# The first keys' tile is loaded earlier and the first unit's maxima are computed among the last projections

## The chip, the cores and the metric

The kernel runs on one core of one Trainium2 chip. The metric is the device time of one execution in microseconds (us); lower is better. The core has TensorE (PE; its weight loads are shown as PEld), VectorE (DVE), ScalarE (ACT), GpSimd (POOL) and SyncE (SP), which here issues nearly all transfers. Each engine works through a queue of its own in order, and semaphores order the engines among each other.

## The reference

Two independent parts read their own inputs, and their outputs are joined on the last axis. L is 2048, D is 448, N is 256, H is 16 heads of 28.

```python
# part A: a diagonal state space convolution
dt = exp(log_dt);  A = -exp(log_A_real) + 1j * A_imag;  C = (C_real + 1j * C_imag) * dt[:, None]
P = exp((A * dt[:, None])[:, :, None] * arange(L))
K = 2.0 * einsum("dn,dnl->dl", C, P).real
y = irfft(rfft(K, 2 * L) * rfft(u.T, 2 * L))[:, :L].T + u * D_skip
# part B: multi-head attention
q, k, v = split(x @ wqkv)
o = softmax(q @ k.T / sqrt(28)) @ v          # for each head
out = concatenate([y, o @ wo], axis=-1)
```

## The kernel before

The attention runs in 16 units, each one head group of 4 heads (g) and a quarter of 512 queries (c). A softmax needs the maximum of each row of scores ahead of the exponentials. The maxima of unit u + 1 are computed while unit u is in its loop, and their negatives are written as two more rows into the q tile of the unit (`qhat<-mh`), so that the score matmul subtracts them. The first unit has no unit ahead of it, so its maxima are computed before the loop starts.

The program has two stages. In the loop (from line 878) the order is written out by hand and kept on all engines. Ahead of it lies a first stage (lines 213 to 565) in which a list scheduler orders the instructions by their place in the program, by their priority and by when their inputs are ready; the builder writes that order into the queue of each engine. Two lines of work share the engines there:

- *Projections.* `work` holds 48 jobs, twelve for each quarter c of the rows of x: eight `qk_proj` (k and q of each head group) and four `v_proj`. A job is 12 matmuls into one of three PSUM buffers (`pm`, handed out by `w_tile`), since x and the weights are split into a high and a low part (`xh`, `xl`; `w_g`, `vh`, `vl`). Its evacuation (`evac`, kept in `pend` until the next job's matmuls are in the program) writes high and low parts into `hl`, or v into one of two tiles `vst`, and stores them to DRAM. For k of the first two quarters it also makes the difference `dhl` by way of `kb`. In the last quarter the v jobs come first.
- *Seeds.* For part A, eight blocks o = 0..7 go through the thirteen steps that `seeds` lists: transposes of `nat`, phases and their reduction (`tri`), sines (the cosine is `sg<-tri,half_pi`), sizes by Exp, products on GpSimd, `g_first` on VectorE, and two stores, `sd<-qhat` and `sd<-sg`. Two `tri` and two `sg` buffers are in turn.

`slots` gives each step of a seed block its stage (four stages from block to block), and `PW` spreads the 48 jobs over 37 stages. `ahead` adds loads at given stages: the key differences `kdif` from stage A0 = 26, the first unit's q at A1 = 34, the first group's k tiles `khat` at the stages KW. The weights of q and k lie in the tile `k0_t`, which is also the first keys' tile: its part j can only be loaded when all projections of head group j are done.

After that stage the first unit's maxima follow (lines 539 to 563): 16 groups of 128 queries of one head. A group has five matmuls of 512 columns into four PSUM banks. The keys are taken in two halves: `kdif` holds differences of keys in pairs, and max(a, b) is relu(a - b) + b. So a group is one Relu over 128x1024 on ScalarE and one custom VectorE instruction that adds, and keeps the maximum. GpSimd supplies -q (`nq`). `max_end` transposes and splits the maxima, `max_put` sends them, and the loop starts. Its first ScalarE copy, `e<-sdb`, reads the first block's seeds back from DRAM.

In the profile every instruction bears line 76, that of the helper through which all engines are called, so the work is told apart by its tiles.

Of the kernel before, what the change touches and what calls it, by code (L numbers as in the profile page):

```python
# [17 lines left out]
L = 2048  # L18
# [22 lines left out]
PS = 1  # L41
SGB, XB, XL = 2, 5, 4
K0, KP, KD, UP = 0, 3.5, 4, 3
A0, A1, KW = 26, 34, (33, 35, 36)

N1 = 32
N2 = 64
# [44 lines left out]
def body(ctx, tc, a, out):  # L92
# [41 lines left out]
    k0_p = pool(k0_st, "k0_p", side="right")  # L134
    k0_t = k0_p.tile([128, HG, L], F32R, name="khat")

    def mm32(o, w, x_, start, stop, at=0):

# [5 lines left out]
    kt_g, kd_g, q_u, m_u, mh_u, o_u, rl_u = {}, {}, {}, {}, {}, {}, {}  # L144

    def load_k(g, j, p):
        if j == 0:
            t = k0_t if g == 0 else p.tile([128, HG, L], F32R, name="khat")
# [62 lines left out]


    with ExitStack() as st:
        sst, xst, wst, mst, psx, psm = (ExitStack() for _ in range(6))
        t_p = pool(sst, "t_p")
        s_p = pool(sst, "s_p")
        x_p = pool(xst, "x_p")
        y_p = pool(wst, "y_p", side="right")
# [17 lines left out]
        nc.gpsimd.memset(k0_t[:CK].rearrange("p g (n e) -> p (g n) e", e=32)[:, :, DH:].bitcast(F32), 0.0)  # L236
# [14 lines left out]
        nats = {}  # L251

        def load_nat(o):
            nats[o] = s_p.tile([PO, 4, 256], F32, name="nat", bufs=2)
# [178 lines left out]
        def transposes(c):  # L433
            for k in range(NCK):
                pt = ps_t.tile([128, CQ], F32, name="pt")[:CK]
                for t in range(4):
                    nc.tensor.transpose(pt[:, t * 128:(t + 1) * 128], xns[c, t // 2][:, t % 2, k * CK:(k + 1) * CK], ident)
                xh[k] = x_p.tile([CK, CQ], F32R, name="xh", bufs=XB)
                xl[k] = x_p.tile([CK, CQ], F32R, name="xl", bufs=XL)
                nc.scalar.activation(xh[k], pt, AF.Copy)  # L440
                nc.vector.tensor_tensor(xl[k], pt, xh[k].bitcast(F32), ALU.subtract)

        def qk_proj(c, s, g):
            pp = w_tile()
# [30 lines left out]
        def v_proj(c, t):  # L475
# [11 lines left out]
                nc.sync.dma_start(v_d[c][:, :, t], vs.rearrange("p (g h) e -> p g (h e)", g=G))  # L487
            return evac

        work = []  # L490
# [20 lines left out]
        for i in range(2):  # L511
            ahead[A1 + i].append(lambda i=i: load_q(0, range(2 * i, 2 * i + 2)))

        for j, t in enumerate(KW):
            ahead[t].append(lambda j=j: load_k(0, j, k0_p))

        def project():

            e = work.pop(0)() if work else None
            while pend:  # L520
                pend.pop(0)()
            if e:
                pend.append(e)

        for t in range(n_stage):
            while work and n_work - len(work) < n_work * (t + 1) / PW:
                project()
            for f in slots[t] + ahead.get(t, []):
                f()
            if t + 1 == PW:  # L530
                project()
                wst.close()
                load_k(0, HG - 1, k0_p)
# [5 lines left out]
        m_p = pool(mst, "m_p")  # L539
        ps_2 = pool(psm, "ps_2", 4, PSUM)  # L540
        nq = m_p.tile([128, HG, CQ], F32R, name="nq")
        m_u[0, 1] = q_p.tile([128, HG * 4], F32, name="m1", bufs=2)
        for i in range(16):
            j, t = divmod(i, 4)
            ts = slice(t * 128, (t + 1) * 128)
            q, kt = q_u[0][:, j, ts], kt_g[0][j]
            if t == 0:
                nc.gpsimd.tensor_scalar(nq[:, j], q_u[0][:, j].bitcast(F32), -1.0, None, op0=ALU.mult)
            pd, pb = (ps_2.tile([128, 2, CQ], F32, name="p2") for _ in range(2))
            kb = kt.rearrange("p (c s n) -> p c s n", c=NQ, s=2)[:, :2, 1, :]  # L550
            mm = nc.tensor.matmul
            mm(pd[:, 0], q, kd_g[0, j], start=True, stop=True)
            mm(pd[:, 1], q, kt[:, 2 * CQ:3 * CQ], start=True, stop=False)
            mm(pd[:, 1], nq[:, j, ts], kt[:, 3 * CQ:], start=False, stop=True)
            mm(pb[:, 0].rearrange("p (c n) -> p c n", c=2), q, kb, start=True, stop=True)
            mm(pb[:, 1], q, kt[:, 3 * CQ:], start=True, stop=True)
            rl = m_p.tile([128, 2, CQ], F32, name="rl2", bufs=2)
            nc.scalar.activation(rl, pd, AF.Relu)
            nc.vector.tensor_tensor_reduce(rl, pb, rl, 1.0, -3.0e38, ALU.add, ALU.max, m_u[0, 1][:, i:i + 1])
        nc.scalar.activation(half_pi[:1], half_pi[:1], AF.Exp)  # L560
        max_end(0, ps_2.tile([128, 2, CQ], F32, name="p2")[:, 0])
        max_put(0)
        psm.close()
        mst.close()
        sst.close()


# [6 lines left out]
    ps_st = ExitStack()  # L574
    ps_g = pool(ps_st, "ps_g", 1, PSUM)
    ps_w[0] = pool(ps_st, "ps_m", 1, PSUM)
    k_pools = [k0_p, kq_p]

    late = [False]

# [577 lines left out]
```

## Time and profile before

| | us |
|---|---|
| median of 3 runs | 1303.82 (1302.89 to 1305.15) |
| the profiled execution | 1307.74 |
| its span, first to last instruction | 1305.7 |
| evacuation of the 43rd projection (k of head group 1, last quarter) on ScalarE | 181.32 |
| first Relu of the maxima | 211.73 |
| end of the last maximum | 235.65 |
| first copy of seeds in the loop | 245.15 |

The profile shows one execution; its 1307.74 us are 3.92 above the median. A row of the timeline is start, duration, engine, line, operation, output tile <- input tiles, shapes and count, and in brackets the idle time ahead of it with what ended it. A row of the waits is who waited for whom, with total, count and longest in us. Matmuls are pipelined, so their durations overlap and their starts give the pace.

### The profile page before, as it was taken

What the parts mean: (1) busy time and instruction counts of PE and PEld (TensorE: products, weight loads), DVE (VectorE), ACT (ScalarE), POOL (GpSimd) and SP (SyncE); (2) the same over time, 40 slices, a digit from 0 to 9 for tenths busy, and PEclk for the clock granted to TensorE, in tenths of its full rate; (3) what the DMA queues carried; (4) which work ended last, traced back from release to release, by engine and by line L of the source; (5) the groups of instructions that cost most, each with busy time, mean ns of one, the idle gap of its engine ahead of it and who ended that gap; (6) DMA issues with size and microseconds to landing.
All of it is one profiled execution on the core that took longest, in us unless ns stands there. A gap on an engine that the chain in (4) does not pass through costs nothing.

```text
span 1305.7 us, 32148 instructions
## 1 busy us (share of the span) xinstructions
PE 1228.7 (94%) x12193; PEld 695.7 (53%) x12193; DVE 907.0 (69%) x2001; ACT 980.3 (75%) x2046; POOL 865.9 (66%) x684
## 2 busy tenths in 40 slices
PE   6888877799999999999999999999997999999998
PEld 5766755355555555555555555555554555545333
DVE  5676656677777787777788888888986555636111
ACT  4877875588888888888788888888886666756463
POOL 2677654478888788888769999999995221424421
PEclk9989887799999999999999999999999999999999
DMA  6677679735866455468634232743324453647666
GB/s 202 207 273 257 218 259 271 212 66 136 185 147 142 109 149 157 142 169 231 162 104 105 56 83 62 157 111 78 82 59 139 146 158 136 203 142 238 202 161 175
DMA packets 200082, 205.28 MB, mean 157 GB/s; under 512 B 95992, under 2 KB 158520, under 8 KB 197880
## 3 DMA queue, kind: packets, MB, share of 16 engines
q1 hardware_dynamic: 199864, 203.22, 56.1%
q8 instruction: 96, 1.57, 0.5%
q14 instruction: 58, 0.48, 0.1%
q10 hardware_dynamic: 64, 0.02, 0.0%
HBM read 120.74 MB, written 82.18 MB: 155 GB/s over the span
## 4 chain that ended last, share of the span: by engine, by line
PE 72%; POOL 8%; ACT 7%; DVE 5%; DMA 4%; issue 4%; SPq 0%; ACTq 0%; POOLq 0%
PE pm L76 39%; PE pss L76 16%; PE po L76 16%; POOL sg L76 2%; POOL e L76 2%; DMA khat<-k 2%; POOL tri L76 2%; ACT tri L76 1%; ACT sg L76 1%; DVE mx L76 1%; POOL p L76 1%; ACT L76 1%; ACT p L76 1%; POOL eu L76 1%; DVE rl L76 1%
## 5 line engine op out<-in xcount | busy, mean ns | idle before, releaser
L76 ACT ACTIVATE p<-pss 128x512 f32<-128x512 f32 x1024 | 560.4, 609 | 109.9 <-PE pss L76 105.9
L76 PE MATMUL pss<-qhat,khat 128*128 128x512 f32 x1024 | 405.7, 402 | 4.0 <-DMA qhat<-mh 2.2
L76 DVE TENSOR_REDUCE mx<-pm 128x1 f32<-128x512 f32 x480 | 308.3, 683 | 121.2 <-PE pm L76 119.5
L76 PE MATMUL pm<-khat,qhat 128*128 128x512 f32 x720 | 314.4, 437 | 6.1 <-ACT rl L76 3.5
L76 POOL TENSOR_TENSOR e<-e,sdb 128x256 f32<-128x256 f32 x168 | 202.0, 1203 | 108.7 <-ACT e L76 67.2
L76 PE MATMUL po<-p,v 128*32 128x512 f32 x2048 | 271.0, 597 | 0.0
L76 POOL TENSOR_TENSOR e<-e,eu 128x256 f32<-128x256 f32 x168 | 248.3, 1478 | 13.2
L76 PEld LDWEIGHTS pm<-khat,qhat 128*128 128x128 f32 x720 | 135.4, 188 | 206.4 <-ACT p L76 47.0
L76 PEld LDWEIGHTS pss<-qhat,khat 128*128 128x128 f32 x1024 | 191.2, 189 | 52.5 <-ACT p L76 13.8
L76 DVE CUSTOM_DVE_ANT_0 rl<-pm,rl 128x512 f32<-128x512 f32 x240 | 165.3, 689 | 70.0 <-ACT rl L76 67.7
L76 POOL TENSOR_TENSOR eu<-e,sdb 128x256 f32<-128x256 f32 x168 | 202.3, 1204 | 0.0
L76 POOL TENSOR_TENSOR p<-pr,pr 64x448 f32<-64x448 f32 x64 | 73.2, 1144 | 155.6 <-PE pm L76 122.3
L76 DVE TENSOR_TENSOR g<-g,zg 128x128 f32<-128x128 f32 x392 | 162.0, 413 | 3.6
L76 ACT ACTIVATE rl<-pm 128x512 f32<-128x512 f32 x240 | 145.3, 605 | 7.7 <-issue 4.1
L76 PE MATMUL pm<-xh,khat 112*128 112x512 f32 x256 | 89.7, 431 | 19.6 <-DVE hl L76 10.6
L76 PE MATMUL pm<-kdif,qhat 128*128 128x512 f32 x240 | 97.0, 404 | 1.7 <-DVE pr L76 1.1
L76 DVE TENSOR_TENSOR zg<-g,zg 128x128 f32<-128x128 f32 x224 | 88.0, 393 | 5.3
L76 PEld LDWEIGHTS pm<-e,g 128*32 128x32 f32 x3584 | 56.9, 110 | 49.2 <-issue 15.7
L76 PE MATMUL pm<-e,g 128*32 128x64 f32 x3584 | 73.6, 223 | 8.7 <-POOL e L76 8.7
L76 ACT ACTIVATE y<-pm 128x448 f32<-128x448 f32 x48 | 26.5, 553 | 59.7 <-PE pm L76 39.1
L76 PEld LDWEIGHTS pm<-xh,khat 112*128 112x128 f32 x256 | 51.0, 205 | 35.9 <-DVE hl L76 12.6
L76 DVE TENSOR_TENSOR pr<-pm,ub 128x448 f32<-128x448 f32 x64 | 37.0, 619 | 46.9 <-PE pm L76 37.7
(133 smaller groups left out, 1491.6 us busy)
## 6 DMA issues: line engine op xcount, KB each, us to landing
sdb<-sd SPq DMA_DIRECT2D x56, 336.0 KB
khat<-k SPq DMA_DIRECT2D x64, 256.0 KB
qhat<-q SPq DMA_DIRECT2D x64, 256.0 KB
sd<-sg SPq DMA_DIRECT2D x8, 1456.0 KB
k<-hl SPq DMA_DIRECT2D x16, 512.0 KB
q<-hl SPq DMA_DIRECT2D x16, 512.0 KB
v<-v SPq DMA_DIRECT2D x32, 256.0 KB
mw<-in_mw SPq DMA_DIRECT2D x16, 512.0 KB
```

The source lines that it names most:

```text
L76: i = f(*args, **kw)
```

## The change

- The weights of q and k get a tile of their own (`w_t`, in a new pool `w_p` on the left). The first keys' tile is opened on the right when the pool of x and v's weights (`y_p`) is closed, that is after the last v job; its loads no longer wait for the projections of q and k.
- In the last quarter the v jobs come after the first k job.
- The low parts of x lie in three buffers of the v pool and one of the x pool.
- The `kdif` loads begin at stage 18, the loads of q at 28. A plan `MG` by number of jobs done gives the k tile to load and the maxima groups to compute: the k tile of head 2 at 41, then head 3, 0, 1; two groups after each of 43 to 50.
- `max_group` works in halves of 512 keys, with `pd` in the transposes' two PSUM buffers (`pt`) and `pb` in the three of the projections. The halves' maxima are joined by one reduction. The negated q lies in `nat` buffers.
- Evacuations of the projections and of the transposes run at a priority raised by 200.

```diff
-A0, A1, KW = 26, 34, (33, 35, 36)
+A0, A1 = 18, 28
+MG = {41: (2, ()), 42: (3, ()), 43: (0, (8, 9)), 44: (1, (10, 11)), 45: (None, (12, 13)), 46: (None, (14, 15)), 47: (None, (0, 1)),
+      48: (None, (2, 3)), 49: (None, (4, 5)), 50: (None, (6, 7))}
+PRI = 200
...
-        w_g = k0_t[:CK].rearrange("p g (i s k h e) -> p i s k g h e", i=2, s=2, k=NCK, h=HG)
+        w_t = w_p.tile([CK, HG, L], F32R, name="w")
+        w_g = w_t.rearrange("p g (i s k h e) -> p i s k g h e", i=2, s=2, k=NCK, h=HG)
...
+        xls = [v_p.tile([128, NK // NQ, HG, 32], F32, name="v", bufs=5).rearrange("p t h e -> p (t h e)")[:CK].bitcast(F32R) for _ in range(3)]
+        xls.append(x_p.tile([CK, CQ], F32R, name="xl"))
...
+                with tc.high_priority(offset=PRI):
+                    nc.scalar.activation(xh[k], pt, AF.Copy)
+                    nc.vector.tensor_tensor(xl[k], pt, xh[k].bitcast(F32), ALU.subtract)
...
+        def max_group(i):
+
+            j, t = divmod(i, 4)
+            ts = slice(t * 128, (t + 1) * 128)
+            if not nqs:
+                m_u[0] = q_p.tile([128, HG, 4, 3], F32, name="mx", bufs=2)
+            if t == 0:
+                if j % 2 == 0:
+                    nq = s_p.tile([128, 4, 256], F32, name="nat", bufs=2).rearrange("p (j a) n -> p j (a n)", j=2).bitcast(F32R)
+                    nqs[j], nqs[j + 1] = nq[:, 0], nq[:, 1]
+                nc.gpsimd.tensor_scalar(nqs[j], q_u[0][:, j].bitcast(F32), -1.0, None, op0=ALU.mult)
+            q, kt = q_u[0][:, j, ts], kt_g[0][j]
+            kb = kt.rearrange("p (c s n) -> p c s n", c=NQ, s=2)[:, :2, 1, :]
+            mm = nc.tensor.matmul
+            for h in range(2):
+                pd, pb = ps_t.tile([128, CQ], F32, name="pt"), w_tile()
+                if h == 0:
+                    mm(pd, q, kd_g[0, j], start=True, stop=True)
+                    mm(pb.rearrange("p (c n) -> p c n", c=2), q, kb, start=True, stop=True)
+                else:
+                    mm(pd, q, kt[:, 2 * CQ:3 * CQ], start=True, stop=False)
+                    mm(pd, nqs[j][:, ts], kt[:, 3 * CQ:], start=False, stop=True)
+                    mm(pb, q, kt[:, 3 * CQ:], start=True, stop=True)
+                rl = kd_p.tile([128, CQ], F32, name="rl", bufs=2)
+                nc.scalar.activation(rl, pd, AF.Relu)
+                nc.vector.tensor_tensor_reduce(rl, pb, rl, 1.0, -3.0e38, ALU.add, ALU.max, m_u[0][:, j, t, h:h + 1])
+
+        def first_maxima(n):
+
+            j, ts = plan.pop(n, (None, ()))
+            if j is not None:
+                if not k0:
+                    yst.close()
+                    k0.append(pool(k0_st, "k0_p", side="right"))
+                load_k(0, j, k0[0])
+            for i in ts:
+                groups.remove(i)
+                max_group(i)
...
-            jobs = v_jobs + jobs if c == NQ - 1 else jobs + v_jobs
+            jobs = jobs[:1] + v_jobs + jobs[1:] if c == NQ - 1 else jobs + v_jobs
...
-            while pend:
-                pend.pop(0)()
+            with tc.high_priority(offset=PRI):
+                while pend:
+                    pend.pop(0)()
             if e:
                 pend.append(e)
+            first_maxima(n_work - len(work))
...
+            elif t + 1 > PW:
+                first_maxima(n_work + t + 1 - PW)
+        while groups:
+            max_group(groups.popleft())
+        nc.scalar.activation(half_pi[:1], half_pi[:1], AF.Exp)
+        m_u[0, 1] = q_p.tile([128, HG * 4], F32, name="m1", bufs=2)
+        nc.vector.tensor_reduce(m_u[0, 1], m_u[0].rearrange("p a b c -> p (a b) c")[:, :, :2], axis=AX.X, op=ALU.max)
+        max_end(0, ps_t.tile([128, CQ], F32, name="pt"))
+        max_put(0)
```

Left out are the removed lines 539 to 563, whose work `max_group` takes over, the pools that go with them, and `nat` tiles of 128 partitions instead of 56.

More of the change, by code (lines that the diff above doesn't have):

```diff
@@ L133, in body @@
     kd_p = pool(att, "kd_p", side="right")
-    k0_p = pool(k0_st, "k0_p", side="right")
-    k0_t = k0_p.tile([128, HG, L], F32R, name="khat")
     def mm32(o, w, x_, start, stop, at=0):
@@ L146, in load_k @@
     def load_k(g, j, p):
-        if j == 0:
-            t = k0_t if g == 0 else p.tile([128, HG, L], F32R, name="khat")
+        if g not in kt_g:
+            t = p.tile([128, HG, L], F32R, name="khat")
             kt_g[g] = [t[:, i] for i in range(HG)]
@@ L213, in body @@
     with ExitStack() as st:
-        sst, xst, wst, mst, psx, psm = (ExitStack() for _ in range(6))
+        sst, xst, wst, yst, psx = (ExitStack() for _ in range(5))
+        k0 = []
         t_p = pool(sst, "t_p")
@@ L217, in body @@
         x_p = pool(xst, "x_p")
-        y_p = pool(wst, "y_p", side="right")
+        w_p = pool(wst, "w_p")
+        y_p = pool(yst, "y_p", side="right")
         ps_w[0] = pool(psx, "ps_w", 1, PSUM)
@@ L253, in load_nat @@
         def load_nat(o):
-            nats[o] = s_p.tile([PO, 4, 256], F32, name="nat", bufs=2)
+            nats[o] = s_p.tile([128, 4, 256], F32, name="nat", bufs=2)[:PO]
             for i, n in enumerate(("A_log_A_real", "A_A_imag", "A_C_real", "A_C_imag")):
@@ L488, in v_proj @@
             return evac
+        nqs, plan = {}, dict(MG)
+        groups = collections.deque([j * 4 + t for j in (2, 3, 0, 1) for t in range(4)])
+        def max_group(i):
[33 more added lines that the diff above has]
+                max_group(i)
         work = []
@@ L512, in body @@
             ahead[A1 + i].append(lambda i=i: load_q(0, range(2 * i, 2 * i + 2)))
-        for j, t in enumerate(KW):
-            ahead[t].append(lambda j=j: load_k(0, j, k0_p))
         def project():
             e = work.pop(0)() if work else None
-            while pend:
-                pend.pop(0)()
+            with tc.high_priority(offset=PRI):
+                while pend:
+                    pend.pop(0)()
             if e:
                 pend.append(e)
+            first_maxima(n_work - len(work))
         for t in range(n_stage):
@@ L532, in body @@
                 wst.close()
-                load_k(0, HG - 1, k0_p)
                 load_q(1)
@@ L536, in body @@
                     load_v(0, c)
+            elif t + 1 > PW:
[7 more added lines that the diff above has]
+        max_put(0)
         xst.close()
         psx.close()
[L539 to L564, printed above, removed]
         sst.close()
@@ L576, in body @@
     ps_w[0] = pool(ps_st, "ps_m", 1, PSUM)
-    k_pools = [k0_p, kq_p]
+    k_pools = k0 + [kq_p]
     late = [False]
```

6 lines of the change are left out of this document (2 added, 4 removed).

## Prediction

> **What bounds the kernel now.** I read the page first. TensorE is the bound over the whole span, so I asked for the busy times by stage to see where it isn't.
>
> ```profile
> span 1305.7 us, 32148 instructions
> ...
> PE 1228.7 (94%) x12193; PEld 695.7 (53%) x12193; DVE 907.0 (69%) x2001; ACT 980.3 (75%) x2046; POOL 865.9 (66%) x684
> ...
> 0.00:200.00 200.00, 163.81 (x705) 128.24 (x705) 128.06 (x207) 143.90 (x247) 118.87 (x97) 0.93 0.72 236
> ...
> 212.00:236.00 24.00, 20.37 (x73) 13.69 (x72) 19.29 (x32) 16.05 (x16) 1.28 (x1) 0.90 1.05 287
> 236.00:246.00 10.00, 4.89 (x10) 2.47 (x10) 2.46 (x6) 1.45 (x4) 0.14 (x1) 0.57 0.81 280
> 246.00:300.00 54.00, 52.35 (x482) 26.83 (x483) 41.57 (x97) 41.79 (x91) 45.71 (x36) 0.95 0.40 91
> ```
>
> (Columns: stretch, length, busy us of PE, PEld, DVE, ACT, POOL, granted clock, DMA share, GB/s.) From 246 us the attention loop keeps TensorE at 52.35 of 54 us, and the change leaves the loop's instructions as they are. All of its effect is in when that loop starts. Ahead of it lie the projections and seeds (to about 207 us), the first unit's maxima (to 236) and a hand-over of 10 us. The chain of waits names the same pieces:
>
> ```profile
> 208.44 9.86 DMA khat<-k
> 218.32 10.46 DMA khat<-k
> ...
> 236.38 5.56 DMA qhat<-mh
> ...
> 242.00 2.99 DMA sdb<-sd
> ```
>
> So some 25 us of maxima stand alone ahead of the loop, with ScalarE busy 16.05 of 24 us. That is what the change tries to cover. The loop's ScalarE queue begins with a copy of the first seeds (e<-sdb), and everything behind it waits for that. My sum therefore carries the start of this copy, 245.15 us now:
>
> ```profile
> 245.15 0.63 ACT L76 ACTIVATE e<-sdb 128x256 f32<-128x256 f32 x1 [6.02 <-DMA sdb<-sd]
> ```
>
> **The change, step by step.** The queues run in order, so I take the queue of each engine from the built program of the changed kernel and put durations of this trace on it. Four facts of that order carry the sum. On ScalarE the cosine of seeds o=5 now stands behind the 43rd projection evacuation (k of head group 1, last quarter); it stood behind the 35th. All of seeds o=6 stand ahead of the first Relu of the maxima. Twenty of the 32 Relus stand ahead of the sines of o=7, whose block lies in the middle of the maxima. On TensorE five projection jobs (q1, k2, q2, k3, q3) lie between the maxima groups.
>
> *A, the 43rd evacuation.* It is at 181.32 us before. The higher priority takes away waits of TensorE for evacuations; between 10 and 180 us these were:
>
> ```profile
> 181.32 0.67 ACT L76 ACTIVATE hl<-pm,kones 128x512 fp32r<-128x512 f32 x1
> ...
> PE pm L76 <- DVE hl L76: 6.6, 5, 2.0
> PE pm L76 <- ACT v L76: 6.3, 5, 3.1
> ...
> PE pm L76 <- DVE kb L76: 3.9, 3, 1.7
> ```
>
> That is 16.8 us at most. The hl and kb rows (10.5) are raised directly; for v, which also waits for its two buffers to be stored, I take a quarter. Gain 12 us, bounds 0 and 16.8 (a loss would need slower evacuations, and they only move forward): A = 169.3.
>
> *B, from there to the first maxima at full flow.* In order: one table load, the step from the cosine of o=5 to that of o=6, then GpSimd's work behind the last cosine up to the first negated q (nq), which the first group's second half reads.
>
> ```profile
> 96.77 0.84 ACT L76 ACTIVATE sg<-tri,half_pi 128x672 f32<-128x672 f32 x1
> ...
> 110.11 0.85 ACT L76 ACTIVATE sg<-tri,half_pi 128x672 f32<-128x672 f32 x1
> ...
> 135.67 0.85 ACT L76 ACTIVATE sg<-tri,half_pi 128x672 f32<-128x672 f32 x1
> ...
> 152.43 0.85 ACT L76 ACTIVATE sg<-tri,half_pi 128x672 f32<-128x672 f32 x1
> ...
> 169.53 1.28 ACT L76 ACT_TABLE_LOAD   x1
> 170.82 0.77 ACT L76 ACTIVATE sg<-tri 128x672 f32<-128x672 f32 x1
> ...
> 174.97 0.86 ACT L76 ACTIVATE sg<-tri,half_pi 128x672 f32<-128x672 f32 x1
> ...
> 196.22 0.86 ACT L76 ACTIVATE sg<-tri,half_pi 128x672 f32<-128x672 f32 x1
> ...
> 200.74 0.66 POOL L76 TENSOR_TENSOR tri<-tri 128x224 f32<-128x224 f32 x1
> ...
> 201.62 3.64 POOL L76 TENSOR_TENSOR qhat<-tri 128x784 f32<-128x784 f32 x2
> ...
> 207.42 5.86 POOL L76 TENSOR_SCALAR nq<-qhat 128x512 fp32r<-128x512 f32 x4 [2.16 <-DMA qhat<-q]
> ```
>
> The cosine step was 16.8 us (135.67 to 152.43), with 13.3 (96.77 to 110.11) and 21.3 (174.97 to 196.22) as bounds. I take 16.8, since nearly the same instructions lie between. Behind the cosine: 196.22 to 201.40, two products of 3.64 together, one nq of 5.86/4 = 1.5, so 10.3. With the table load B = 1.3 + 16.8 + 10.3 = 28.4, and the maxima flow from 169.3 + 28.4 = 197.7. The k tiles they need are loaded by then: their issue waits for the last v matmul and for o=5's store, both well ahead. So the 20 us of DMA khat<-k leave the chain, and what is late next is the seeds.
>
> *C, the maxima themselves.* Before, 211.73 to the last read at 235.65, 23.9 us, a stall for k included:
>
> ```profile
> 211.73 1.94 ACT L76 ACTIVATE rl<-p 128x1024 f32<-128x1024 f32 x2 [4.59 <-PE p L76]
> ...
> 235.57 0.08 DVE L76 DVE_READ_ACCUMULATOR2_ANT m<- 128x1 f32 x1
> ...
> L76 DVE CUSTOM_DVE_ANT_0 rl<-p,rl 128x1024 f32<-128x1024 f32 x16 | 19.2, 1224 | 8.3 <-ACT rl L76 7.8
> ...
> L76 DVE CUSTOM_DVE_ANT_0 rl<-pm,rl 128x512 f32<-128x512 f32 x240 | 165.3, 689 | 70.0 <-ACT rl L76 67.7
> ...
> 190.75 0.63 PE L76 MATMUL pm<-xh,khat 112*128 112x512 f32 x2
> ...
> 191.45 0.63 PE L76 MATMUL pm<-xh,khat 112*128 112x512 f32 x2
> ```
>
> In halves a group costs VectorE 2 x 0.689 instead of 1.224, which adds 16 x 0.15 = 2.5 us; the stall (1.2 to 1.6 us) goes. I keep 23.9.
>
> *D, the five projections.* Three matmuls start every 0.70 us (190.75 to 191.45), so a job of 12 takes 2.8 us, and five take 14.0. Their evacuations hardly overlap a group: the job's pm buffer is freed by a maximum of the group before, and the next group's Relu waits behind the job. That is 14.0 on the path.
>
> *E, the block of o=7.* From its first sine input at 192.08 to the last copy at 206.20 it took 14.1 us before.
>
> ```profile
> 192.08 0.76 ACT L76 ACTIVATE sg<-tri 128x672 f32<-128x672 f32 x1
> ...
> 205.64 0.56 ACT L76 ACTIVATE sg<-px 128x112 f32<-128x112 f32 x2 [1.49 <-DVE sg L76]
> ```
>
> The last projection's 2.8 runs beside it: 11.3 on the path. Bounds 5 (the maxima fill its waits for GpSimd and VectorE) and 17 (it also waits for o=5's buffer, whose store now stands in SyncE's queue behind k of group 3: 1456 KB, some 5 us).
> The Trainium skill, "ScalarE: Activation LUTs", What ACT_TABLE_LOAD costs, gives each change of table about 1.38 us of draining on top of a load of 1.28. Here the load takes 1.28 and the next instruction starts 0.01 us behind it (169.53, 170.82). By the page the three loads of this block would make it 4.1 us longer, 1323.6 us in all; the trace decides, and I add nothing.
>
> Together the last maximum is at 197.7 + 23.9 + 14.0 + 11.3 = 246.9, against 235.65: 11.3 us late.
>
> *F, the hand-over.* Before, 235.65 to 245.15, 9.5 us. Now the order of stores changes:
>
> ```profile
> 242.00 1.28 SPq L76 DMA_DIRECT2D sdb<-sd  x3
> ...
> SPq L76 <- DMA qhat<-mh: 7.7, 1, 7.7
> ...
> 236.00:238.00 2.00, 0.88 (x3) 0.41 (x3) 0.56 (x2) 0.00 (x0) 0.00 (x0) 0.84 1.08 379
> ...
> sd<-qhat SPq DMA_DIRECT2D x8, 896.0 KB
> ...
> sd<-sg SPq DMA_DIRECT2D x8, 1456.0 KB
> ```
>
> Each transfer of the built program waits for the one eight back on its semaphore; here the first seed load waits for the maxima's transfer qhat<-mh (the 7.7 us). In the changed program the last v load (256 KB) and, through it, o=7's two stores wait for qhat<-mh too, and the seed load is queued behind them. At 379 GB/s these 2608 KB take 7.0 us in front of it. In return qhat<-mh no longer follows the stores: 5.56 us falls toward the 2.99 of the seed load, 2.6 less. Net 4.4 late, bounds 0 (the loads pass the stores) and 7. [...]
>
> *Edits at nothing.* The four low halves of x keep four buffers, as before (three of them idle v buffers). The kdif loads move up by eight stages among the v stores; DMA engines are busy 0.72 of 0 to 200 us, and if that room were gone, 1 MB at 236 GB/s is 4.3 us. The two negated q tiles take idle nat buffers. The added join of two columns is one VectorE instruction, under the 0.7 us of a maximum.
>
> Sum: 11.3 + 4.4 = 15.7 us late. The profiled execution took 1307.74 us (span 1305.7) and becomes 1323.4; it lies 3.9 above the median of 1303.82, to which I add the same: **1319.5 us**. Bounds: A -4.8/+12, B -3.5/+4.5, E -6.3/+5.7, F -4.4/+2.6. As independent errors they combine to -10 and +14, so this case alone gives 1310 to 1334.
>
> **The rivals.** *It covers the maxima after all.* All 16.8 us of A are gained (164.5), B goes in its shortest step (24.9), the maxima run at TensorE's own rate under the projections (16 x 5 x 0.233 + 14.0 = 32.7) with 5 for o=7: 227.1, and the hand-over stays 9.5. The loop's copy is then at 236.6, 8.5 us earlier: 1295.3. For it: ScalarE and VectorE have a third of 0 to 200 us free. Against it: it needs every term at its good end, and the order of o=7's block is fixed. It decides as soon as the last maximum comes ahead of some 231 us. *Gains and losses cancel*, A at its best and F at nothing: 15.7 - 4.8 - 4.4 - 6.3 = 0.2, so 1304. *SyncE's queue holds back k's last two tiles.* Four of these loads stand behind the stores of q2 and q3, and the groups that need them wait; the earlier loads took 9.86 and 10.46 us. One such wait adds 10: 1329.5. That the maxima don't move isn't open, since the built order shows it.
>
> **How the numbers follow.** Forecast 0.63, covered 0.20, cancel 0.05, k held back 0.12. A measurement of this kernel can tell about 0.2% (2.6 us) from no change. Faster 0.20, same 0.05, slower 0.75. For 8 in 10 the range reaches down to the covered case and up to the end of the forecast's own: 1296 to 1334.
>
> **What would show it.** Right: the 43rd evacuation near 169 us, the first Relus of the maxima near 198, a pause of them of some 10 us around the sines of o=7, the last maximum near 247, and e<-sdb starting 13 to 15 us behind it. Wrong: Relus flowing ahead of 190 us, a last maximum ahead of 235, or a seed load that lands within 4 us of its issue although o=7's stores were issued just ahead of it.

## The result: 1341.3 us, 2.9% slower, and the profile after

| | before | after |
|---|---|---|
| median, us | 1303.36 (1302.15 to 1305.15) | 1341.3 (1340.1 to 1342.91) |
| ratio of after to before, 95% interval | | 1.0291 (1.0273 to 1.0309) |
| first copy of seeds in the loop, us from the span's start | 245.15 | 282.97 |
| end of the last Relu of the maxima | 234.39 | 268.77 |

The forecast was 1319.5 (1296 to 1334): the sign was right, the time lies above the range, and the loss was 37.9 us where 15.7 were forecast. All of it lies where the prediction looked for it: the loop starts 37.8 us later. From there to the end of the span it takes 1057.9 us, against 1060.6 before.

The busy times by stage of after (length, busy us of PE, PEld, DVE, ACT, POOL, granted clock, DMA share, GB/s), to be read against the prediction's rows of before:

```profile
0.00:200.00 200.00, 146.56 (x648) 116.47 (x648) 119.34 (x195) 139.13 (x235) 103.02 (x89) 0.89 0.72 228
200.00:212.00 12.00, 1.59 (x4) 1.27 (x5) 4.90 (x12) 4.41 (x10) 11.75 (x11) 0.50 0.13 28
212.00:236.00 24.00, 22.82 (x84) 16.38 (x82) 11.68 (x33) 11.01 (x19) 2.72 (x2) 0.90 0.33 107
236.00:260.00 24.00, 10.91 (x35) 7.38 (x36) 8.83 (x24) 14.29 (x21) 7.58 (x5) 0.74 0.89 280
260.00:285.00 25.00, 12.87 (x30) 7.67 (x29) 10.56 (x30) 7.50 (x17) 1.24 (x3) 0.57 0.67 209
```

By 200 us TensorE has done 648 matmuls, where it had done 705 before. It was to do more. From 200 to 212 us it is busy for only 1.59 us while GpSimd works for 11.75, and from 236 to 285 it stands still for half of the time. The timeline of TensorE names the waits, that of GpSimd the work they wait for:

```profile
186.48 1.10 PE L79 MATMUL pn<-ident,nat 56*128 56x56 f32 x8 [14.89 <-ACT nat L79]
194.21 0.77 PE L79 MATMUL pt<-kdif,qhat 128*128 128x512 f32 x1 [6.63 <-DMA qhat<-q]
198.78 0.77 PE L79 MATMUL pm<-khat,qhat 128*128 128x512 f32 x1 [3.81 <-DMA khat<-k]
210.41 0.79 PE L79 MATMUL pt<-khat,nat 128*128 128x512 f32 x1 [10.43 <-POOL nat L79]
...
237.97 0.47 PE L79 MATMUL pm<-khat,qhat 128*128 128x512 f32 x1 [2.54 <-DMA khat<-k]
```

```profile
205.25 3.65 POOL L79 TENSOR_TENSOR qhat<-tri 128x784 f32<-128x784 f32 x2
208.87 5.85 POOL L79 TENSOR_SCALAR nat<-qhat 128x512 fp32r<-128x512 f32 x4
249.44 1.64 POOL L79 TENSOR_TENSOR sg<-sg 128x672 f32<-128x672 f32 x1 [34.72 <-ACT sg L79]
```

The first maxima stand in TensorE's queue ahead of five projections. They wait for the negated q, which stands in GpSimd's queue behind the products of seeds o=6 and o=7. So the projections wait for seeds, and after that GpSimd has nothing to do for 34.72 us. The timeline of ScalarE carries the prediction's steps:

```profile
174.00 0.68 ACT L79 ACTIVATE hl<-pm,kones 128x512 fp32r<-128x512 f32 x1
...
176.00 0.85 ACT L79 ACTIVATE sg<-tri,half_pi 128x672 f32<-128x672 f32 x1
...
200.00 0.84 ACT L79 ACTIVATE sg<-tri,half_pi 128x672 f32<-128x672 f32 x1
...
209.92 0.64 ACT L79 ACTIVATE rl<-pt 128x512 f32<-128x512 f32 x1
...
217.93 0.60 ACT L79 ACTIVATE hl<-pm 128x512 fp32r<-128x512 f32 x1 [3.96 <-PE pm L79]
...
244.54 0.76 ACT L79 ACTIVATE sg<-tri 128x672 f32<-128x672 f32 x1 [3.58 <-DMA sd<-sg]
245.21 0.58 ACT L79 ACTIVATE hl<-pm 128x512 fp32r<-128x512 f32 x1
...
249.37 1.28 ACT L79 ACT_TABLE_LOAD   x1
250.66 0.85 ACT L79 ACTIVATE sg<-tri,half_pi 128x672 f32<-128x672 f32 x1
...
268.17 0.60 ACT L79 ACTIVATE rl<-pt 128x512 f32<-128x512 f32 x1 [0.50 <-PE pt L79]
...
282.97 0.63 ACT L79 ACTIVATE e<-sdb 128x256 f32<-128x256 f32 x1 [10.62 <-DMA sdb<-sd]
```

Between the evacuations at 174.00 and 217.93 there is none. Of the prediction's signs, the pause of the Relus around the sines of o=7 came (11.5 us, from 240.97 to 252.45) and the copy 13.5 us behind the last maximum; the 43rd evacuation, the first Relus and the last maximum were 5, 12 and 23 us later than it had them. Transfers suffer too: between 187 and 240 us the kernel before moves 14.78 MB and the kernel after 7.10. These are the totals of that window in the views of the transfers, before first, then after:

```profile
DMA packets 7487, 14.78 MB, mean 279 GB/s; under 512 B 624, under 2 KB 4028, under 8 KB 6971
```

```profile
DMA  9999999999800000000000000960039300696269
...
DMA packets 3102, 7.10 MB, mean 134 GB/s; under 512 B 321, under 2 KB 1383, under 8 KB 2715
```

In the first row each digit is the busy tenths of the transfer engines in 1/40 of the window: from about 202 to 220 us nothing moves, since SyncE's queue stands at a store of the next projection. What was not moved there has to be moved later, ahead of the loop.

### The profile page after: what moved, and what is told of

Its sections match the earlier page's. It is cut to its first block, busy times and chain, and to the rows that moved or that the text cites. A ratio compares the mean times of both kernels' runs of the same rounds, so it can differ in the third digit from the quotient of the medians.

```text
span 1340.9 us, 32223 instructions
## 1 busy us (share of the span) xinstructions
PE 1227.3 (92%) x12193; PEld 695.7 (52%) x12193; DVE 906.7 (68%) x2034; ACT 991.5 (74%) x2068; POOL 860.2 (64%) x684
## 4 chain that ended last, share of the span: by engine, by line
PE 74%; POOL 8%; ACT 5%; DVE 4%; DMA 4%; issue 4%; SPq 0%; ACTq 0%; POOLq 0%; DVEq 0%
PE pm L79 41%; PE pss L79 16%; PE po L79 15%; POOL sg L79 2%; POOL e L79 2%; POOL tri L79 1%; DMA tri<-in_B_wqkv 1%; DVE mx L79 1%; ACT L79 1%; POOL p L79 1%; PE pt L79 1%; ACT tri L79 1%; ACT p L79 1%; DMA qhat<-q 1%; POOL qhat L79 1%
## 5 line engine op out<-in xcount | busy, mean ns | idle before, releaser
L79 PE MATMUL pm<-khat,qhat 128*128 128x512 f32 x752 | 330.3, 440 | 22.1 <-ACT rl L79 9.6
L79 PEld LDWEIGHTS pm<-khat,qhat 128*128 128x128 f32 x752 | 142.8, 190 | 226.7 <-ACT p L79 51.1
L79 DVE CUSTOM_DVE_ANT_0 rl<-pm,rl 128x512 f32<-128x512 f32 x272 | 186.7, 689 | 90.1 <-ACT rl L79 84.7
L79 PE MATMUL pm<-xh,w 112*128 112x512 f32 x256 | 86.8, 422 | 11.7 <-DVE hl L79 7.9
L79 POOL TENSOR_TENSOR sg<-sg 128x672 f32<-128x672 f32 x16 | 26.8, 1672 | 76.3 <-ACT sg L79 66.0
L79 ACT ACTIVATE y<-pm 128x448 f32<-128x448 f32 x48 | 26.5, 553 | 59.1 <-PE pm L79 37.4
```

The lines of the kernel that those rows point to most:

```text
L79: i = f(*args, **kw)
```

## The experiments

One table holds all kernels. Times of stages are us from the span's start, read on ScalarE: the first Relu of the maxima, the end of the last, the first copy of seeds. The gap is the difference of the last two. The kernel before ran again beside each group of kernels (medians 1303.3 to 1304.3), and the ratio is to that run. Behind the seed copy the span takes 1057.9 to 1063.0 us in every kernel, so the copy carries the time to within some 5 us.

| kernel | median | ratio to before (95%) | first Relu | last Relu ends | seed copy | gap |
|---|---|---|---|---|---|---|
| before | 1303.4 | | 211.7 | 234.4 | 245.2 | 10.8 |
| after | 1341.3 | 1.0291 (1.0273 to 1.0309) | 209.9 | 268.8 | 283.0 | 14.2 |
| no_priority | 1325.75 | 1.0171 (1.0155 to 1.0187) | 196.7 | 252.0 | 265.7 | 13.8 |
| maxima_at_end | 1325.17 | 1.0167 (1.0147 to 1.0186) | 210.9 | 251.2 | 266.0 | 14.8 |
| no_priority_at_end | 1324.34 | 1.0161 (1.0144 to 1.0178) | 205.0 | 260.1 | 263.6 | 3.5 |
| before_priority | 1306.06 | 1.0015 (1.0005 to 1.0024) | 215.6 | 237.0 | 244.9 | 7.9 |
| seeds_priority | 1328.01 | 1.0198 (1.0174 to 1.0221) | 212.8 | 262.8 | 266.3 | 3.5 |
| stores_priority | 1345.41 | 1.0317 (1.0299 to 1.0335) | 214.7 | 280.0 | 286.6 | 6.6 |
| groups_later | 1333.78 | 1.0230 (1.0215 to 1.0246) | 210.6 | 260.1 | 274.3 | 14.2 |
| put_other_queue | 1335.13 | 1.0240 (1.0224 to 1.0256) | 207.2 | 265.7 | 270.4 | 4.7 |
| old_maxima_early_k | 1326.25 | 1.0174 (1.0153 to 1.0196) | 237.4 | 258.9 | 262.7 | 3.8 |
| old_maxima_late_k | 1316.53 | 1.0103 (1.0078 to 1.0128) | 225.6 | 249.9 | 253.7 | 3.8 |
| halves_late_k | 1319.56 | 1.0115 (1.0094 to 1.0136) | 207.3 | 255.7 | 259.2 | 3.5 |
| interleave_late_k | 1325.95 | 1.0168 (1.0152 to 1.0183) | 203.8 | 252.3 | 265.7 | 13.5 |
| order_before_early_kd | 1312.98 | 1.0075 (1.0058 to 1.0092) | 225.9 | 245.9 | 249.7 | 3.8 |
| own_tile_alone | 1306.97 | 1.0033 (1.0022 to 1.0044) | 220.4 | 241.8 | 245.6 | 3.8 |
| own_tile_halves | 1305.36 | 1.0015 (1.0006 to 1.0024) | 215.4 | 240.2 | 243.7 | 3.5 |
| own_tile_put_other_queue | 1308.70 | 1.0042 (1.0027 to 1.0057) | 221.2 | 241.2 | 244.3 | 3.1 |
| halves_q_stage_33 | 1311.23 | 1.0053 (1.0038 to 1.0067) | 211.5 | 235.8 | 249.3 | 13.5 |
| halves_q_stage_32 | 1310.25 | 1.0050 (1.0037 to 1.0062) | 208.4 | 238.9 | 252.4 | 13.5 |

### Priority and interleaving, each alone

`no_priority`: the with-block around `xh` and `xl` goes in the same way.

```diff
-            with tc.high_priority(offset=PRI):
-                while pend:
-                    pend.pop(0)()
+            while pend:
+                pend.pop(0)()
```

> The kernel after, with its evacuations at the ordinary priority again; the own tile, the halves and the maxima between projections stay. Theory (the raised priority puts the seed blocks o=5 to o=7 behind the evacuations, and the maxima wait behind them): the cosines of o=6 come less than 18 us after those of o=5, the maxima start before 205 us, and some 8 to 20 of the 37.9 us come back: 1320 to 1333 us. Rival (maxima in halves between projections cost by themselves, priority is harmless): within 4 us of the kernel after, 1337 to 1345 us.

`before_priority` puts the same two blocks into the kernel before.

> The kernel before with nothing but the two with-blocks of higher priority (200) around the evacuations. Theory (priority starves the seeds): the sines of o=7 come after the last evacuation of a projection, the stores of o=7 later than 234 us, and the time rises by 8 to 25 us: 1311 to 1328 us. Rival (the evacuations come sooner and the seeds are hidden): 1298 to 1304 us.

`maxima_at_end`:

```diff
+MG = {41: (2, ()), 42: (3, ()), 43: (0, ()), 44: (1, ())}
```

> The kernel after with the four loads of k's tile where they are and no group of maxima among the projections: all 16 follow the last job in program order. Theory (late seeds set the start of the loop, not the place of the maxima): o=7's block still ends late, 1330 to 1350 us. Rival (groups between projections are what costs): the projections end by 225 us as before, the maxima take some 25 us behind them, 1300 to 1318 us.

`no_priority_at_end` has both reversals.

> The kernel after with both reverted: ordinary priority, and all 16 groups behind the last job; the own tile, the early loads of k and the halves stay. Theory (two separate costs, 16 us each as the single reversals gave): 1304 to 1314 us. Rival (both reversals undo the same stall, the maxima held behind late seeds): 1319 to 1327 us.

Priority alone costs almost nothing: 0.15% (0.05 to 0.24). In `before_priority` the projections are done 17 us sooner (189.24 against 206.54), the seeds 8 us later (o=7's cosine at 204.23 against 196.22), and the loop starts when it did; the 1311 us expected were wrong, and 1306.06 lies between theory and rival:

```profile
189.24 0.58 ACT L76 ACTIVATE hl<-pm 128x512 fp32r<-128x512 f32 x1
...
215.60 1.02 ACT L76 ACTIVATE rl<-p 128x1024 f32<-128x1024 f32 x1 [1.39 <-PE p L76]
...
244.93 0.65 ACT L76 ACTIVATE e<-sdb 128x256 f32<-128x256 f32 x1 [3.71 <-DMA sdb<-sd]
```

Either reversal takes 16 us off the kernel after (in the range of the theory for `no_priority`, between theory and rival for `maxima_at_end`), and both together take 17, not 32; that is in the range of the rival of `no_priority_at_end`. The table shows why. The last Relu ends at 268.8 with priority and interleaving, 251.2 with priority alone, 252.0 with interleaving alone, 260.1 with neither. So under the raised priority interleaving costs 17.5 us, and under the ordinary one it gains 8.1. There the seeds are not late when the first maxima need GpSimd: the cosine of o=6 is at 183.01, the first Relu at 196.69. The step from o=5's cosine (162.65) was still 20.4 us, not under 18. The gain is then lost in the gap, 13.8 us against 3.5, to which I come below. The theory expected a sum where the two interact. The cosine of o=6 shows the same: it comes at 174.97 before, at 183.32 with the priority alone, at 183.01 with the rest of the change alone, and at 200.00 with both.

### Which line of work to raise, and how late the groups

`seeds_priority` (on top of `no_priority`), and `stores_priority` (on top of after, the same block around `put_e` and `put_g`):

```diff
-            for f in slots[t] + ahead.get(t, []):
-                f()
+            with tc.high_priority(offset=PRI):
+                for f in slots[t]:
+                    f()
+            for f in ahead.get(t, []):
+                f()
```

> The kernel after with the raised priority taken from the evacuations and given to the steps of the seed blocks; the maxima stay among the projections. Theory (the late seed blocks cost it): o=7's stores land before the last maximum, the seed copies of the loop wait for nothing of o=7, and the start of the loop comes back to between 235 and 252 us: 1294 to 1311 us. Rival (the interleaving itself or the smaller tiles cost it): over 1320 us.

> The kernel after with the raised priority also on the two stores of each seed block. Theory (o=7's block stands amid the maxima because its buffer is released by o=5's store, which stands behind k's store of group 3; there it costs ScalarE some 14 us and a cold TensorE): o=7's block comes ahead of all but one of the Relus, the first maxima start 5 to 8 us later but run through, the copies of the loop don't wait for o=7: 1318 to 1330 us. Rival (the block costs the same wherever it stands): 1337 us or more.

Both theories failed on the time. With the seeds raised, o=7's cosine comes at 194.82 and the seed copy waits for nothing; but now the projections starve, and 1328.0 is on the rival's side (over 1320). The first row is this kernel's first 100 us, the second that of before (261 matmuls against 349):

```profile
0.00:100.00 100.00, 65.77 (x261) 50.56 (x262) 60.97 (x112) 67.72 (x124) 56.39 (x56) 0.85 0.61 199
```

```profile
0.00:100.00 100.00, 81.25 (x349) 63.51 (x350) 65.62 (x112) 67.41 (x121) 55.01 (x55) 0.95 0.70 229
```

With the stores raised, o=7's block does come ahead of all but one Relu, as expected; but q's loads now stand in SyncE's queue behind a store of seeds that isn't ready, and TensorE does only seven matmuls between 200 and 231 us, with the projections behind them. The last of its three waits is for a Relu that stands behind o=7's block in ScalarE's queue. 1345.4 is on the rival's side:

```profile
211.95 0.76 PE L79 MATMUL pt<-kdif,qhat 128*128 128x512 f32 x1 [11.98 <-DMA qhat<-q]
216.88 0.77 PE L79 MATMUL pm<-khat,qhat 128*128 128x512 f32 x1 [4.17 <-DMA khat<-k]
231.68 0.79 PE L79 MATMUL pt<-khat,qhat 128*128 128x512 f32 x1 [11.90 <-ACT rl L79]
```

`groups_later`:

```diff
+MG = {41: (2, ()), 42: (3, ()), 43: (0, ()), 44: (1, ()), 46: (None, (8, 9)), 47: (None, (10, 11)), 48: (None, (12, 13)),
+      49: (None, (14, 15)), 50: (None, (0, 1))}
```

> The kernel after with the first two groups of maxima ordered three jobs later (after job 46, not 43) and two a job from there, the rest behind the last job. Theory (TensorE's queue: the first maxima stand ahead of four projections and wait for negated q behind two seed blocks on GpSimd): the projections of q1 to q2 no longer wait for them, the last evacuation comes before 222 us instead of 245, and the time comes to that of the maxima at the end or a little below: 1318 to 1327 us. Rival (only the number of groups that remain behind the last job counts): 1332 us or more.

The last evacuation came at 224.53, not 245.21, and the last Relu 8.7 us sooner, so maxima in front of projections in TensorE's queue do hold them up. But the time came down by 7.5 us only: 1333.8 is not in the theory's range (1318 to 1327) but in that of the rival (1332 or more), and the edit also leaves more groups behind the last job, so it doesn't separate the two.

### The hand-over

```diff
-            (nc.sync if u else nc.scalar).dma_start(
+            (nc.sync if u else nc.gpsimd).dma_start(
```

> The kernel after with the two transfers of the first unit's maxima into its q tile issued by GpSimd instead of ScalarE; no wait of SP's last stores and loads then stands on them. Theory (the hand-over: the loop's seed copies are loaded behind o=7's stores, which wait for the maxima): the first seed copy of the loop comes some 9 to 10 us after the last maximum and not 13.5, so 3 to 5 us come back: 1336 to 1338.5 us. Rival (the bandwidth of the loads ahead sets it, or the first scores do): 1340 to 1343 us.

The place was right, the size was not: the gap fell from 14.2 to 4.7, further than the theory had it, and 6.2 us came back by the medians (1335.13, just below the 1336 to 1338.5 expected). This is the gap of after in SyncE's timeline:

```profile
256.88 15.86 SPq L79 DMA_DIRECT2D v<-v  x4
272.83 0.39 SPq L79 DMA_DIRECT2D sd<-qhat  x1
273.32 0.50 SPq L79 DMA_DIRECT2D sd<-sg  x1
273.88 4.40 SPq L79 DMA_DIRECT2D sdb<-sd  x3
```

The last v load waits for `qhat<-mh`, since in the built program a transfer waits for the one eight back. Stores and seed loads follow it. The first seed copy then waits for its load; the row of after stands above, this is that of `put_other_queue`:

```profile
270.39 0.63 ACT L79 ACTIVATE e<-sdb 128x256 f32<-128x256 f32 x1 [2.21 <-DMA sdb<-sd]
```

The column of gaps splits by this in all kernels. Where the built order makes o=7's stores wait for `qhat<-mh`, the gap is 13.5 to 14.8 us (after, `no_priority`, `maxima_at_end`, `groups_later`, `interleave_late_k`, both `halves_q`). Where only a seed load waits for it, 6.6 to 10.8 (before, `before_priority`, `stores_priority`). Where neither does, 3.1 to 4.7. The slot in the count of eight follows from how many transfers the scheduler happens to place ahead. It moves the gap by 10 us. Only `put_other_queue` takes the wait away by one edit; the other kernels are sorted by their built order.

### The loads of k, the halves and the order of the jobs

`old_maxima_early_k` has both reversals and the old full-width maxima block in place of `while groups`. `old_maxima_late_k` then moves the loads, and `halves_late_k` is `no_priority_at_end` with them:

```diff
+MG = {45: (0, ()), 46: (1, ()), 47: (2, ()), 48: (3, ())}
```

> The kernel with both reversals, and the maxima as before besides: 16 full-width groups in PSUM and SBUF pools opened behind the last projection. Own tile, order of the last quarter and loads of k after jobs 41 to 44 stay. Theory (o=5's last store, which frees the buffer for o=7's sines, stands behind 12 loads of k in SP's queue; o=7's first sine holds ScalarE and with it the last evacuations): the sine still waits some 8 us, 1316 to 1325 us. Rival (the halves and shared PSUM cost it): 1300 to 1312 us.

> The same with the four loads of k after jobs 45 to 48, so that o=5's last store stands ahead of all of them in SP's queue. Theory (store behind the loads of k): o=7's first sine comes at 197 to 204 us without that wait, the last evacuation of a projection before 220 us, 1303 to 1312 us. Rival (the place of the loads doesn't matter): within 3 us of the kernel with early loads.

> No raised priority, all maxima in halves behind the last job, loads of k after jobs 45 to 48. Theory (the place of the loads): 8 to 18 us below the same with the loads after jobs 41 to 44 (1324.3 us), that is 1306 to 1316 us, and above the full-width maxima with late loads by 2 to 5 us (1.42 us a group in halves against 1.28). Rival (halves or PSUM): 1319 us or more.

The place of the loads is worth 9.7 us in full width and 4.8 in halves, both less than expected. 1326.25 is 1.3 us above the first theory's range, with the wait of 8.21 us that it named. 1316.53 lies between theory and rival: the sine came when expected, the last evacuation at 222.86 and not before 220. 1319.56 is on the rival's side (1319 or more), though 3.0 us above the full width as the theory had it. With early loads, o=5's last store is issued behind 12 of the 16, and o=7's first sine waits for its buffer. These are the rows of SyncE and ScalarE with early loads, then with late ones, where the store goes out at 196.05 and the sine runs straight behind the evacuation:

```profile
199.74 2.43 SPq L78 DMA_DIRECT2D khat<-k  x4
202.21 0.46 SPq L78 DMA_DIRECT2D sd<-sg  x1
```

```profile
205.85 0.60 ACT L78 ACTIVATE hl<-pm 128x512 fp32r<-128x512 f32 x1 [9.59 <-DMA q<-hl]
214.66 0.76 ACT L78 ACTIVATE sg<-tri 128x672 f32<-128x672 f32 x1 [8.21 <-DMA sd<-sg]
```

```profile
202.87 0.60 ACT L78 ACTIVATE hl<-pm 128x512 fp32r<-128x512 f32 x1 [7.41 <-PE pm L78]
203.36 0.76 ACT L78 ACTIVATE sg<-tri 128x672 f32<-128x672 f32 x1
```

`interleave_late_k` puts eight groups back among the last jobs:

```diff
+MG = {45: (0, ()), 46: (1, ()), 47: (2, ()), 48: (3, (0, 1)), 49: (None, (2, 3)), 50: (None, (4, 5, 6, 7))}
```

> As the last, with eight groups of maxima ordered among the last three jobs. Theory (interleaving is worth nothing while TensorE's queue holds the first maxima ahead of projections and the seeds set ScalarE's order): within 4 us of the same with all groups at the end. Rival (interleaving pays once the loads don't block the store): 6 us or more below it.

It is 6.4 us slower, outside both. The last Relu ended 3.4 us sooner, and the gap grew from 3.5 to 13.5: again a gain of interleaving that the hand-over takes away.

`order_before_early_kd` (on `old_maxima_late_k`) and `own_tile_alone` (on that) undo what is left:

```diff
-            jobs = jobs[:1] + v_jobs + jobs[1:] if c == NQ - 1 else jobs + v_jobs
+            jobs = v_jobs + jobs if c == NQ - 1 else jobs + v_jobs
-A0, A1 = 18, 28
+A0, A1 = 18, 34
...
-A0, A1 = 18, 34
+A0, A1 = 26, 34
```

> The kernel with full-width maxima at the end, late loads of k and no raised priority, and now the jobs of the last quarter in their old order (four v jobs first, then k and q) with the loads of q back at stage 34. Loads of kd still from stage 18. Theory (order: the v evacuations behind a seed block left TensorE without a free PSUM buffer, 7.41 us before q1's evacuation): 1303 to 1310 us. Rival (loads of kd, or the own tile): 1314 us or more.

> The last with the loads of kd back at stage 26: ScalarE's instructions now stand in the order of the kernel before, and what is left of the change is the own tile for the weights, x's low parts in v's buffers and the loads of k that no longer wait for the last projection. Theory (the tile itself is harmless and saves the waits for k, at most 4 us of the 24.6 us of maxima): 1299 to 1304.5 us. Rival (x's low parts in v's buffers or the tile's place cost something): 1306 us or more.

The order of jobs, together with q's loads at stage 34, is worth 3.5 us (1303 to 1310 us were expected, 1312.98 came: between theory and rival). The place of the `kdif` loads is worth 6.0, which the prediction had at nothing. The own tile alone is not faster than before; at 1306.97 it is 0.33% slower (0.22 to 0.44), on the rival's side (1306 or more). Its loop starts only 0.4 us later than that of before; what the rest of the 3.6 us is, and whether the tile's place or x's low parts cost it, no run shows. The view of its transfers between 187 and 240 us bears on why an earlier load of k brings nothing here, with the first group's wait on TensorE and on GpSimd below it:

```profile
DMA packets 7573, 14.90 MB, mean 281 GB/s; under 512 B 618, under 2 KB 4178, under 8 KB 7058
```

```profile
216.19 0.77 PE L78 MATMUL p<-kdif,qhat 128*128 128x512 f32 x1 [17.09 <-DMA khat<-k]
```

```profile
216.08 5.85 POOL L78 TENSOR_SCALAR nq<-qhat 128x512 fp32r<-128x512 f32 x4 [12.09 <-DMA k<-hl]
```

These 14.90 MB against 14.78 before, at 281 and 279 GB/s, are the same work at the same rate. What goes first only pushes something else back: the last two loads of q are issued behind 12 of k (at 205.31, where before issued them at 199.76 behind 4), and the first group, which needs them, starts at 216.19 and not at 207.49. The brackets name other transfers, but q is what the two instructions, which start within 0.1 us of each other, both read.

The steps from after to before add up to the 37.9 us: 17.0 for priority and interleaving, 9.7 for the place of k's loads, 6.0 for that of the `kdif` loads, 3.5 for the order of the jobs with q's loads, 3.6 for the own tile, and -1.9 for the halves, which is not clear of the noise. So more than half of the loss (20.9 us) is there without priority and interleaving. Each step was taken back in one order only; where steps interact, another order would divide them otherwise.

`own_tile_halves` is `own_tile_alone` with the `while groups` block of after in place of the full-width one, and `own_tile_put_other_queue` is `own_tile_alone` with the same one-line edit of the queue as `put_other_queue`.

> The last with the maxima in halves, in the PSUM buffers of the projections, behind the last job. Theory (a group takes 1.42 us in halves against 1.28, 16 groups): 1 to 4 us above the own tile alone. Rival (halves start sooner, since no pool has to be opened behind the last projection): 1 to 5 us below it.

> The own tile alone, and the two transfers of the first unit's maxima issued by GpSimd. Theory (hand-over): the seed copies are loaded without a wait for the maxima, 1 to 3 us below the own tile alone, and with it below the kernel before: 1297 to 1302 us. Rival (there the loads are not the last to come): within 1 us of the own tile alone.

With the halves, 1.6 us below the own tile alone (the rival), hardly more than the noise: the first Relu comes 5.0 us sooner, and the rival's reason is that no pool has to open behind the last projection. Moving the transfers of the maxima brought nothing: 1308.70 is 1.7 us above the own tile alone, against the theory and a little outside the rival. In the own tile's built order the seed copy does not wait for them in the first place (gap 3.8).

### The order of the loads

`halves_q_stage_33` takes `own_tile_halves`, A1 = 33, and the groups in the order of the loads; `halves_q_stage_32` has A1 = 32.

```diff
-        groups = collections.deque([j * 4 + t for j in (2, 3, 0, 1) for t in range(4)])
+        groups = collections.deque([j * 4 + t for j in (0, 1, 2, 3) for t in range(4)])
```

> The own tile with halves at the end, q's two loads one stage earlier (33, not 34), the groups taken in the order in which k is loaded (parts 0 to 3). Theory (the first group waited until 214.6 us for loads standing behind others: k's part 2 in the halves, q in the full width): the first Relu comes at 205 to 211 us instead of 215.4, and the time 2 to 6 us below the halves of before (1305.4): 1299 to 1303.5 us. Rival (the loads are bound by bandwidth, 16.8 MB between 185 and 250 us, and the last part of k comes as late as ever): 1303.5 to 1306.5 us.

> The same with q's loads two stages earlier (32): the first two stand ahead of all of k's, and TensorE's queue holds six half groups ahead of the last projection. Theory (loads' order): within 2 us of the last. Rival (interleaving costs again, since the last projection now waits for loads of k): 3 to 8 us above it.

The maxima came sooner and the time did not. In the first the first Relu is at 211.45 instead of 215.37 (211 at most was expected) and the last ends at 235.8, 4.4 us sooner than in `own_tile_halves`; the gap took 10.0 back, and 1311.23 is above theory and rival. `halves_q_stage_32` lies 1.0 us below it, as its theory had it:

```profile
235.17 0.60 ACT L78 ACTIVATE rl<-pt 128x512 f32<-128x512 f32 x1 [0.34 <-PE pt L78]
...
249.27 0.63 ACT L78 ACTIVATE e<-sdb 128x256 f32<-128x256 f32 x1 [9.85 <-DMA sdb<-sd]
```

No kernel that ran beats the one before. This order of loads together with the transfers on GpSimd's queue was not tried. With a gap of 4.7 its seed copy would be at 240.5, 4.7 us ahead of before; that is an estimate from two runs. It carries no time, since the span behind the copy differs by up to 5 us and the built program may answer otherwise.

## Why the prediction was wrong, point by point

- *Where it would act*: right. The loop's start carries all of the 37.8 us.
- *A, the 43rd evacuation at 169.3*: 174.00. The waits for evacuations between 10 and 180 us fell from 16.8 to 13.9 us (DVE hl 7.9, DVE kb 3.6, ACT v 2.4), so a gain of 2.9 where 12 were taken. It came 7.3 us earlier, inside the bounds of 0 and 16.8; where the other 4.4 us come from I can't say.
- *B, 28.4 us to the first maxima*: 36.4. This is the first step that failed, outside its bounds (24.9 to 32.9). Its last part was exact: 200.00 to 210.33 for the first negated q is 10.3. What was mis-sized is the step from cosine to cosine: 24.0 us, where 16.8 were taken between 13.3 and 21.3. The rows of before already spoke against that bound: from 152.43 to 174.97 the step is 22.5, from 110.11 to 135.67 it is 25.6, and I passed over both. In after the exponentials of o=7's `nat`, its transposes and its phases stand between the two cosines, and ScalarE waits there for GpSimd's part of the seeds, 2.38 us at 181.19 and 3.17 at 191.05. In other kernels this step takes 19.1 (`before_priority`), 20.4 (`no_priority`) and 25.6 (`maxima_at_end`).

```profile
181.19 0.39 ACT L79 ACTIVATE tri<-tri 128x224 f32<-128x224 f32 x1 [2.38 <-POOL tri L79]
...
191.05 1.04 ACT L79 ACTIVATE tri<-tri 128x1008 f32<-128x1008 f32 x1 [3.17 <-POOL tri L79]
```

- *"The k tiles they need are loaded by then"*: wrong by 3.81 us for the first, which did not set the time, since the negated q came 11.6 us later still, and by 2.54 at 237.97. That later wait is the place of the rival that priced it at 10.
- *C, D and E, 49.2 us of maxima, projections and o=7's block*: from 210.4 to the last maximum's end at 269.5, 59.1. This failed too: 9.9 us more, where the bounds allowed 5.7. The wait for o=5's buffer, which only a bound had held, is in the chain of waits: the store takes 7.08 us from its issue, ScalarE stands 3.58. The rest I can't divide exactly. The last five groups took 11.1 us (257.67 to 268.77), 2.2 each, against 1.43 in `no_priority_at_end`: about 4 us, in which both the low clock (granted 0.57 between 260 and 285 us) and the copies of o=7's block between the groups may have a part.

```profile
237.43 7.08 DMA sd<-sg
...
270.49 1.87 DMA qhat<-mh
...
273.88 9.07 DMA sdb<-sd
```

- *F, the hand-over, 13.9 us in all*: 13.5, for the reason given: the seed load took 9.07 us behind o=7's stores and 2.99 before, 6.1 more where 7.0 were taken, and `qhat<-mh` took 3.7 less where 2.6 were taken. Another 1.5 us, from its landing at 272.36 to the issue of the seed load at 273.88, were not in the sum; that the total came so near is in part luck. The Trainium skill, "DMA: Bandwidth & Descriptors", Queues, rings and completion order, has the descriptors of a ring taken in order, though a later one may finish its write first. The trace agrees with the order: the load took about as much longer as the stores' 2352 KB need at the 379 GB/s of the prediction's row, 6.4 us by estimate.
- *Nothing added for draining*: right. The table loads of o=7's block cost 1.28 each with the next instruction 0.01 behind (249.37 to 250.65, then 250.66).
- *Edits at nothing*: the earlier `kdif` loads were not free. They measured 6.0 us, in a kernel without priority and interleaving, near the 4.3 that the prediction named for the case that the room is gone.

The errors are 4.7 in A, 8.0 in B, 9.9 in C to E, -0.4 in F: 22.2 us. B and C to E share a fault: I priced each queue's order with durations taken where the other queues ran more freely. The seeds were late since projections went first and o=7's work stood between, TensorE stood since its queue held maxima that waited for those seeds, and SyncE's queue stood at the stores of projections that TensorE had not reached.

## What to carry to other kernels

When work that waits is moved ahead of work that doesn't, in a queue that runs in order, ask what its last input stands behind on that input's engine, and price the wait of all that follows it. Ahead of moving a load forward, look whether the transfers are already full there: here 14.8 and 14.9 MB went at 279 and 281 GB/s in two orders. And where transfers share a few semaphores in turn, an edit anywhere can move a wait from one transfer to another; here that moved the hand-over by 10 us, and the one edit that took it away gave 6.2 us back.

## What the runs showed of the hardware

Idle TensorE pays twice. The granted clock was 0.50 between 200 and 212 us, behind waits of 14.89, 6.63 and 3.81 us and with one of 10.43 in it. It was 0.57 between 260 and 285, behind waits that ended at 253.08 (6.01 us) and 258.30 (3.08 us) and with one of 8.27 in it. Matmuls of 512 columns then start every 0.43 us instead of every 0.23; behind the wait of 2.54 us at 237.97 they still started every 0.23. The first two rows stand behind the wait that ended at 210.41, the other two show the pace that followed:

```profile
211.00 0.63 PE L79 MATMUL pm<-khat,qhat 128*128 128x512 f32 x1
211.43 0.63 PE L79 MATMUL pt<-kdif,qhat 128*128 128x512 f32 x1
...
217.73 0.40 PE L79 MATMUL pt<-kdif,qhat 128*128 128x512 f32 x1
217.96 0.40 PE L79 MATMUL pm<-khat,qhat 128*128 128x512 f32 x1
```

The Trainium skill, "TensorE: Matmul & The Clock Gate", HAM oscillation, warns of gaps of over some 3.4 us; the trace agrees with it.
